# Seven products for tiles 2 and 3 as well, with prepared units kept in DRAM and retention beside the first two second layers

## The chip, the core and the metric

The kernel runs on one core of a Trainium2 chip. The metric is the device time of one execution in microseconds (us), median of the runs. TensorE (PE) multiplies, VectorE (DVE), ScalarE (ACT) and GpSimd (POOL) do the elementwise work, SyncE (SP) issues most transfers; POOL issues some too.

## The reference: what is computed

A retention layer over 4 batches, 8 heads, 768 tokens and head size 64 is followed by two feed-forward networks over the 3072 tokens:

```python
for t in range(S):                                   # retention, per head
    state = gamma * state + outer(k[t], v[t])
    y[t] = q[t] @ state / sqrt(D)
x = y as (3072, 512)
h = x @ w_in                                         # 512 -> 2048
g = where(h >= 1, h, where(h <= -1, 0, (h + 1)**2 / 4))
x = g @ w_out                                        # 2048 -> 512
out = ((x @ w1) * (x @ w2) @ w3) @ w_out2            # 512 -> 1024 -> 1024 -> 512
```

The weights arrive as 64-bit floats.

## The kernel before, in words

**Tiles.** The 3072 tokens are six tiles of 512 (a tile is one chunk of 128 tokens of each of the four batches). Retention of a chunk is one piece of scores on TensorE (`qk_ops`), a mask on VectorE, and one piece of values (`pv_ops`), which also brings the chunk's keys times values for the next state. Its result is the tile's x.

**Precision.** Every product of float32 values is made of three: each operand is split into a high and a low part (`plan_split`: a ScalarE copy gives the high part, a VectorE subtraction the low one), and `mm3` multiplies high by high, low by high and high by low. The 64-bit weights are converted on ScalarE and VectorE first (`convert`: a raw load, two ScalarE and four VectorE instructions).

**First layer, direct** (`plan_h`, tiles 0 to 3). For each of 16 blocks f of 128 hidden features, four blocks of x by `mm3`, that is twelve products of 128x512, then the gate: two ScalarE and one VectorE instruction on `r`. For tiles 0 to 3 (`LATE = 4`) the gated block is stored to DRAM (`g_d`, from POOL), loaded again (from SP) when its second layer comes, and split.

**First layer, seven products** (`plan_x_pair`, `plan_hu`, tiles 4 and 5). Two tiles and two blocks f form a 2x2 block product that is done with seven products of half the depth in place of eight (Strassen's scheme, in Winograd's form). The operands of x are sums and differences of the two tiles (`xops`, 14 buffers of the pool `w`); the operands of the weights are a *unit*, made from two blocks of w_in by sums on VectorE and splits (`plan_unit`, in the two buffers `xh` and `xl`). One unit n gives blocks 2n and 2n + 1 for both tiles. Tile 4's gate goes straight to its split; tile 5's blocks wait in `g_last`.

**Second layer** (`plan_y`). y of a tile sums over the 16 blocks f into four banks, twelve products a step. Tile 0 takes the converted w_out (`wo0`), which is also stored split (`wo_d`); later tiles load it back. Tiles 3 and 2 share one load a step. After step 15 the four banks are evacuated to DRAM (`plan_evac`).

**Second network.** w1, w2 and w3 are converted in the background and stored (`background`), w3 and w_out2 are multiplied into one matrix (`plan_w3o`, after tile 5's second layer), and the rest works by pairs of tiles (`plan_ab`, `plan_out`). The change does not touch that last part.

**Order.** The list `pe` gives TensorE's order by hand. A planner (`Plan`) lets each instruction of the other engines be issued in the order of its due time, taken back from the TensorE steps that need it, with the buffers of each pool counted; `bound` and `floor` move a due time. TensorE may take one of the next `AHEAD = 12` entries of its list if an earlier one is not ready. In time: retention of chunks 0 and 1 and h of tiles 0 and 1, with chunk 2 near the end; h of tile 2 alternating with y of tile 0; h of tile 3 alternating with y of tile 1, with chunks 3 to 5 between; y of tiles 3 and 2; the units of tiles 4 and 5 with y of tile 4 two steps behind; y of tile 5; w3 with w_out2; the pairs.

Of the kernel before, what the change touches and what calls it, by code (L numbers as in the profile page):

```python
# [15 lines left out]
P = 128  # L16
# [12 lines left out]
LATE = 4  # L29
PAIR = 4  # L30
KEEP = 260.0
DIRECT = 0
FEW = 4
# [17 lines left out]
class Op:  # L51
    def __init__(self, eng, cost, fn, size=0.0):
        self.eng, self.cost, self.fn, self.size = eng, cost, fn, size
        self.deps, self.after, self.vals = set(), [], []
        self.due = self.bound = float("inf")
        self.pos = self.end = None
        self.floor = -float("inf")
        self.store = False

    def lag(self):  # L60
        return self.size / 335.0 + 2.0 if self.size else 0.1


class Plan:
# [72 lines left out]
    def emit(self, begin):  # L137
# [18 lines left out]
        while done < len(self.ops):  # L156
# [71 lines left out]
def retention_then_two_ffns(  # L228
# [36 lines left out]
        (i, f): dram.tile([P, TT], F32, name=f"g_d{i}_{f}") for i in range(LATE) for f in range(NF1)  # L265
# [23 lines left out]
    def new_r(name):  # L289
# [10 lines left out]
    def convert(width, load, finish, after=(), bound=None, floor=-1e9, to=None):  # L300
# [22 lines left out]
        if to:  # L323
            words = lambda: to.ap.rearrange("p h w -> p (h w)").bitcast(U32)
        else:
            to, words = u, lambda: u.ap
        plan.op("DVE", 0.17 + 0.53 * s, lambda: nc.vector.scalar_tensor_tensor(
            out=words(), in0=odd(), scalar=0xC0000000, in1=u.ap,
            op0=ALU.bitwise_and, op1=ALU.bitwise_or), r=[raw, u], w=[to], bound=bound)
        finish(to)  # L330
# [77 lines left out]
    for f, n in [(0, 1), (1, 1)] + [(f, 2) for f in range(2, NF1, 2)]:  # L408
        convert(512 * n, load_rows(w_out[f // 2][:, f % 2 * 512:f % 2 * 512 + 512 * n]), finish_wo(f, n))
# [10 lines left out]
    background += [(load_rows(w3t[j]), [("w3", j), ("w3", NF2 + j)]) for j in range(DIRECT, NF2)]  # L420
# [20 lines left out]
    def new_ps(c):  # L441
        if c < 3:
            return Val("pe", lambda: psum["e"].tile([P, 2, 512], F32, tag="pa", name="pe"))
# [5 lines left out]
    def chunk(b, c):  # L449
# [10 lines left out]
        if c < 3:  # L460
# [3 lines left out]
        else:  # L464
            v_ = Val("v", lambda: att.tile([P, H, D], F32, tag="v", name="v"))
            k_ = Val("k", lambda: att.tile([P, H, D], F32, tag="k", name="k", bufs=1))
# [5 lines left out]
        ps = new_ps(c)  # L472

        def scores():
            q_t, k_t = q_at(), kT_at()
            for p in range(NP):
                for h in range(2):
                    r = slice(64 * h, 64 * h + 64)
                    nc.tensor.matmul(
                        out=ps.ap[:, h, p * C:(p + 1) * C], lhsT=k_t[r, p, :], rhs=q_t[r, p, :],  # L480
# [3 lines left out]
        qk = qk_ops[b, c] = plan.op("PE", 0.95, scores, w=[ps], use=[q_, kT_], after=[lq, lk])  # L484
# [6 lines left out]
        plan.op("DVE", 1.25, lambda: nc.vector.tensor_tensor(  # L491
            out=a_at().rearrange("p h a t -> p (h a) t"),
            in0=ps.ap.rearrange("p h (a t) -> p (h a) t", a=NP),
            in1=mask.rearrange("p h a t -> p (h a) t"), op=ALU.mult,
        ), r=[ps], w=[a])
# [49 lines left out]
        if c >= PAIR:  # L545
# [49 lines left out]
    hs, gs, h_ops, y_ops = {}, {}, {}, {}  # L595

    def plan_h(i, f):
# [13 lines left out]
        if i < 2:  # L611
# [8 lines left out]
        kept = r  # L620
        if i < LATE:
            d = Val(None, None)
            plan.op("POOL", 1.0, lambda: nc.gpsimd.dma_start(out=g_d[i, f], in_=r.ap), r=[r], w=[d], size=256)
            kept = Val("st", lambda: new_st("g"))
            plan.op("SP", 0.43, lambda: nc.sync.dma_start(out=kept.ap, in_=g_d[i, f]), r=[d], w=[kept], size=256)
# [12 lines left out]
    def keep_win(f, after, bound):  # L638
# [5 lines left out]
            r=[w], w=[t], after=after, bound=bound).floor = bound - 20.0  # L644
        plan.op("POOL", 0.6, lambda: nc.gpsimd.dma_start(
            out=win_d[f // 2][:, 512 * (f % 2):512 * (f % 2) + 512], in_=t.ap), r=[t], w=[d], size=256).floor = bound - 18.0

    def plan_unit(u, src, kept, after=()):
# [3 lines left out]
        plan.op("SP", 0.45, lambda: nc.sync.dma_start(out=u.ap, in_=src), r=kept, w=[u], size=512, after=after)  # L652
# [17 lines left out]
    def unit_tiles():  # L670
        return [xpool.tile([P, NK, TT], F32R, tag=t, name="unit") for t in ("xh", "xl")]
# [13 lines left out]
    def plan_x_pair():  # L685
        for kb in range(2):
            x4, x5 = xs[PAIR, kb], xs[PAIR + 1, kb]

            def operand(name, x, h):
                t = xops[kb, name] = Val("w", lambda: new_w("xop"))  # L690
# [23 lines left out]
    g_last = [Val("g5", lambda: late[0].tile([P, 2, 512], F32, tag="wc", name="g5", bufs=NF2)) for _ in range(NF1 // 2)]  # L714
    hu_ops = {}

    def plan_hu(n):
        uh, ul = plan_unit(
            Val("u", lambda: cpool.tile([P, 1024], F32, tag="u", name="u")),
            win_d[n], [win_kept[2 * n], win_kept[2 * n + 1]])  # L720
# [3 lines left out]
        ops = hu_ops[n] = []  # L724

        def product(name, where, first):
            def fn():
                w = views((uh.ap, ul.ap))[name]
                for kb in range(2):
                    x = xops[kb, name].ap  # L730
# [7 lines left out]
            ops.append(plan.op("PE", 1.362, fn, r=[uh, ul, xops[0, name], xops[1, name]],  # L738
# [8 lines left out]
        def gate(f, src, src_at, second):  # L747
# [4 lines left out]
            if second:  # L752
                g = g_last[f // 2]
# [7 lines left out]
            gs[PAIR, f] = g, plan_split(g, r, (slice(None),))  # L761
# [25 lines left out]
    def y_banks(i, beside):  # L787

        if not beside:
            vals = [Val("acc", lambda: psum["acc"].tile([P, TT], F32, tag="acc", name="y1acc")) for _ in range(NK)]  # L790
            return [(v, lambda v=v: v.ap) for v in vals]
        hs = [Val("h", lambda: ps_h.tile([P, TT], F32, tag="h", name="y1acc")) for _ in range(2)]
        pair = Val("pa", lambda: psum["a"].tile([P, 2, 512], F32, tag="pa", name="y1acc"))
        return [*((v, lambda v=v: v.ap) for v in hs), *((pair, lambda j=j: pair.ap[:, j]) for j in range(2))]

    def plan_y(tiles, f):

        if tiles[0] == 0:
            w = wo0[f]
        else:  # L800
            w = Val("wo", lambda: new_wo("wo"))
            plan.op("SP", 0.45, lambda: nc.sync.dma_start(out=w.ap.bitcast(F32), in_=wo_d[f]),
                    r=[wo_kept[f]], w=[w], size=512)
        for n, i in enumerate(tiles):
            if f == 0:
                banks[i] = y_banks(i, n < len(tiles) - 1)
            if i == PAIR + 1:
                g = Val("wo", lambda: new_wo("g"))
                plan_split(g, g_last[f // 2], (slice(None), f % 2))
            else:  # L810
                g, _ = gs.pop((i, f))

            def fn(i=i, g=g):
                for m, (_, at) in enumerate(banks[i]):
                    mm3(
                        at(), w.ap[:, 0, m * P:(m + 1) * P], w.ap[:, 1, m * P:(m + 1) * P],
                        g.ap[:, 0, :], g.ap[:, 1, :], f == 0, f == NF1 - 1,
                    )

            y_ops[i, f] = plan.op("PE", 2.724, fn, r=[g, w], w=list(dict.fromkeys(v for v, _ in banks[i])))  # L820
        if f == NF1 - 1:
            for i in tiles:
                for m, (v, at) in enumerate(banks[i]):
                    if 0 < i < PAIR:
                        if m % 2 == 0:
                            st = Val("w", lambda: wpool.tile([P, 2, 512], F32, tag="w", name="y1st"))
                        y1_stored[i, m] = plan_evac(y1_d[i][m], v, at, m, st, lambda st=st, m=m: st.ap[:, m % 2, :])
                    else:
                        st = Val("st", lambda: new_st("y1st"))
                        y1_stored[i, m] = plan_evac(y1_d[i][m], v, at, m, st, lambda st=st: st.ap)  # L830
# [7 lines left out]
    def plan_evac(dst, ps, at, m, st, st_at):  # L838
        done = Val(None, None)
        plan.op("ACT" if m % 2 else "DVE", 0.63, lambda: evacuate(st_at(), at(), m), r=[ps], part=[st, done])  # L840
# [19 lines left out]
    def plan_w3o(u):  # L860
        hf, j = divmod(u, NF2)
        if j == 0:
            banks["w3", hf] = y_banks(None, False)
# [5 lines left out]
        def fn():  # L869
            for m, (_, at) in enumerate(banks["w3", hf]):  # L870
                mm3(
                    at(), t.ap[:, 0, m * P:(m + 1) * P], t.ap[:, 1, m * P:(m + 1) * P],
                    t2.ap[:, 0, :], t2.ap[:, 1, :], j == 0, j == NF2 - 1,
                )

        w3_ops[u] = plan.op("PE", 2.724, fn, r=[t, t2], w=[v for v, _ in banks["w3", hf]])
        if j == NF2 - 1:
            for m, (v, _) in enumerate(banks["w3", hf]):
# [121 lines left out]
    with tc.manual_schedule():  # L1000
# [39 lines left out]
        for i in range(LATE):  # L1040
            for f in range(NF1):
                plan_h(i, f)
        for tiles in ((0,), (1,), (3, 2)):
            for f in range(NF1):
                plan_y(tiles, f)
        for f in range(2):
            keep_win(f, [y_ops[1, f]], KEEP + 9.0 * f)
        plan_x_pair()
        for n in range(NF1 // 2):
            plan_hu(n)  # L1050
        for i in (PAIR, PAIR + 1):
            for f in range(NF1):
                plan_y((i,), f)
# [24 lines left out]
        pieces = [x[b, 2] for b in range(B) for x in (qk_ops, pv_ops)]  # L1078
        lagging = 0
        for f in range(2, NF1):  # L1080
# [6 lines left out]
            if f >= NF1 - 3:  # L1087
                pe.append(pieces.pop(0))
        for f in range(lagging, NF1):
# [177 lines left out]
```

## Time and profile before

| | |
|---|---|
| median of 3 runs | 1025.09 us (1024.82 to 1025.96) |
| the profiled execution | 1026.57 us |
| its span | 1024.8 us |
| mean granted TensorE clock | 0.998 |

The span runs from the first to the last instruction in the profile; the profiled execution's time is 1.8 us longer. TensorE's products are pipelined: one shows as 0.39 us while the next starts 0.23 us after it. So the starts tell the cost, not the durations. An instruction's idle time before it stands in brackets with what ended it.

### The profile page before, as it was taken

What the parts mean: (1) busy time and instruction counts of PE and PEld (TensorE: products, weight loads), DVE (VectorE), ACT (ScalarE), POOL (GpSimd) and SP (SyncE); (2) the same over time, 40 slices, a digit from 0 to 9 for tenths busy, and PEclk for the clock granted to TensorE, in tenths of its full rate; (3) what the DMA queues carried; (4) which work ended last, traced back from release to release, by engine and by line L of the source; (5) the groups of instructions that cost most, each with busy time, mean ns of one, the idle gap of its engine ahead of it and who ended that gap; (6) DMA issues with size and microseconds to landing.
All of it is one profiled execution on the core that took longest, in us unless ns stands there. A gap on an engine that the chain in (4) does not pass through costs nothing.

```text
span 1024.8 us, 14489 instructions
## 1 busy us (share of the span) xinstructions
PE 1004.5 (98%) x5444; PEld 819.0 (80%) x5444; DVE 691.0 (67%) x1053; ACT 503.1 (49%) x845; POOL 96.0 (9%) x125
## 2 busy tenths in 40 slices
PE   6899999999999999999999999999999999999998
PEld 4777878878887788888888787888888888888886
DVE  6787569843656476687776867576884778747750
ACT  2467556632434454357766744444452445434430
POOL 2122332222323200000000000000000000000000
PEclk9999999999999999999999999999999999999999
DMA  9998959956998878864545784111321120311002
GB/s 269 261 272 252 330 177 365 365 194 207 374 343 304 313 265 294 318 213 163 185 185 211 254 300 159 44 39 42 113 89 66 42 103 32 134 41 42 21 4 79
DMA packets 71483, 191.23 MB, mean 187 GB/s; under 512 B 8946, under 2 KB 9330, under 8 KB 69492
## 3 DMA queue, kind: packets, MB, share of 16 engines
q1 hardware_dynamic: 63536, 164.39, 47.2%
q0 software_dynamic: 7584, 25.70, 6.5%
q8 instruction: 43, 0.70, 0.3%
q14 instruction: 28, 0.23, 0.1%
q10 hardware_dynamic: 292, 0.20, 0.1%
HBM read 139.93 MB, written 50.33 MB: 186 GB/s over the span
## 4 chain that ended last, share of the span: by engine, by line
PE 93%; DMA 3%; DVE 1%; ACT 1%; issue 1%; SPq 0%; ACTq 0%; DVEq 0%
PE bank_a L934 13%; PE y1acc L276 10%; PE y1acc L277 10%; PE y1acc L278 10%; PE bank_b L934 6%; PE hps L276 6%; PE hps L278 5%; PE hps L277 5%; PE oacc L982 4%; PE oacc L981 4%; PE oacc L983 4%; PE bank L733 4%; PE banks L733 3%; PE bank_c L934 3%; DMA raw<-in_w_in_dram 2%; PE pa L532 2%
## 5 line engine op out<-in xcount | busy, mean ns | idle before, releaser
L276 PE MATMUL y1acc<-g,wo 128*128 128x512 f32 x384 | 151.3, 394 | 1.1 <-ACT g L337 0.6
L278 PE MATMUL y1acc<-g,wo 128*128 128x512 f32 x384 | 149.7, 390 | 0.4 <-DVE g L339 0.4
L277 PE MATMUL y1acc<-g,wo 128*128 128x512 f32 x384 | 149.6, 390 | 0.0
L934 PE MATMUL bank_a<-yop,unit 128*128 128x512 f32 x576 | 145.7, 389 | 0.0
L934 PEld LDWEIGHTS bank_a<-yop,unit 128*128 128x128 f32 x576 | 108.1, 188 | 22.5
L276 PE MATMUL hps<-xh,win 128*128 128x512 f32 x256 | 102.8, 402 | 4.0 <-DVE r L618 2.1
L278 PE MATMUL hps<-xl,win 128*128 128x512 f32 x256 | 100.7, 393 | 0.0
L277 PE MATMUL hps<-xh,win 128*128 128x512 f32 x256 | 100.6, 393 | 0.0
L942 ACT COPY c<-bank_a 128x512 f32<-128x512 f32 x72 | 42.3, 587 | 98.0 <-PE bank_a L934 95.7
L615 ACT ACTIVATE r<-hps 128x512 f32<-128x512 f32 x64 | 38.2, 597 | 106.3 <-PE hps L278 104.9
L276 PEld LDWEIGHTS y1acc<-g,wo 128*128 128x128 f32 x384 | 72.1, 188 | 18.7 <-ACT g L337 1.1
L278 PEld LDWEIGHTS y1acc<-g,wo 128*128 128x128 f32 x384 | 72.1, 188 | 15.8 <-DVE g L339 0.8
L277 PEld LDWEIGHTS y1acc<-g,wo 128*128 128x128 f32 x384 | 72.1, 188 | 14.4
L337 ACT CAST g<-g 128x512 fp32r<-128x512 f32 x80 | 48.7, 620 | 65.8 <-PE y1acc L278 57.4
L618 DVE SCALAR_TENSOR_TENSOR r<-hps,r 128x512 f32<-128x512 f32 x64 | 43.9, 687 | 53.2 <-ACT r L617 52.4
L658 DVE TENSOR_TENSOR unit<-unit_w,unit 128x512 fp32r<-128x512 f32 x96 | 59.0, 622 | 28.3 <-ACT unit L656 27.9
L981 PE MATMUL oacc<-wc,p 128*128 128x512 f32 x192 | 74.7, 389 | 0.0
L982 PE MATMUL oacc<-wc,p 128*128 128x512 f32 x192 | 74.7, 389 | 0.0
L983 PE MATMUL oacc<-wc,p 128*128 128x512 f32 x192 | 74.7, 389 | 0.0
L934 PE MATMUL bank_b<-yop,unit 128*128 128x512 f32 x288 | 73.1, 389 | 0.0
L656 ACT CAST unit<-unit_w 128x512 fp32r<-128x512 f32 x96 | 53.6, 568 | 28.4 <-PE bank_b L934 14.6
L934 PEld LDWEIGHTS bank_b<-yop,unit 128*128 128x128 f32 x288 | 54.1, 188 | 11.2
(166 smaller groups left out, 1789.9 us busy)
## 6 DMA issues: line engine op xcount, KB each, us to landing
wo<-wo_d SPq DMA_DIRECT2D x64, 512.0 KB, 5.6
g_d<-r POOLq DMA_DIRECT2D x64, 256.0 KB, 4.8
g<-g_d SPq DMA_DIRECT2D x64, 256.0 KB, 5.3
unit_w<-sp_wab SPq DMA_DIRECT2D x24, 512.0 KB, 3.4
wo_d<-wo POOLq DMA_DIRECT2D x16, 512.0 KB, 7.3
raw<-in_w_dram SPq DMA_DIRECT2D x16, 512.0 KB, 6.4
raw<-in_w3t_dram SPq DMA_DIRECT2D x8, 1024.0 KB, 7.3
raw<-in_w_in_dram SPq DMA_DIRECT2D x28, 256.0 KB, 7.9
```

The costliest lines, as they stand in the source:

```text
L276: nc.tensor.matmul(out=ps, lhsT=lh, rhs=rh, start=first, stop=False)
L277: nc.tensor.matmul(out=ps, lhsT=ll, rhs=rh, start=False, stop=False)
L278: nc.tensor.matmul(out=ps, lhsT=lh, rhs=rl, start=False, stop=last)
L337: plan.op("ACT", 0.63, lambda: nc.scalar.copy(out=dst.ap[:, 0, :], in_=at()), r=r, w=[dst, hi], use=use, bound=bound)
L618: plan.op("DVE", 0.7, lambda: nc.vector.scalar_tensor_tensor(out=r.ap, in0=ps.ap, scalar=1.0, in1=r.ap, op0=ALU.max, op1=ALU.min), r=[ps], ...
L656: plan.op("ACT", 0.18 + 0.00088 * (b - a), lambda: nc.scalar.copy(out=hi(), in_=u.ap[:, a:b]), r=[u], part=[v, done])
L658: plan.op("DVE", 0.15 + 0.00106 * (b - a), lambda: nc.vector.tensor_tensor(out=lo(), in0=u.ap[:, a:b], in1=hi(), op=ALU.subtract), r=[u, d ...
L733: nc.tensor.matmul(out=at[where](), lhsT=l, rhs=r, start=first and kb + k == 0, stop=kb == 1 and k == 2, skip_group_check=True,)
L934: nc.tensor.matmul(out=vals[where].ap, lhsT=l, rhs=r, start=first and kb + k == 0, stop=kb == 1 and k == 2, skip_group_check=True,)
L981: nc.tensor.matmul(out=ps.ap, lhsT=lh, rhs=wh, start=(f == 0), stop=False)
L982: nc.tensor.matmul(out=ps.ap, lhsT=lh, rhs=wl, start=False, stop=False)
L983: nc.tensor.matmul(out=ps.ap, lhsT=ll, rhs=wh, start=False, stop=(f == NF2 - 1))
```

## The change

- `LATE` goes; the direct first layer is left for tiles 0 and 1. Tiles 2 and 3 take the seven products too: `plan_x_pair(i)` and `plan_hu(i, n)` run for i = 2 and i = 4.
- In the pass for tiles 2 and 3 a unit is prepared as before and both its buffers are stored to DRAM (`store_unit`, seven parts of 256 KB); in the pass for tiles 4 and 5 it is loaded ready made (`load_unit`).
- x of tiles 4 and 5 is stored to DRAM when it is complete and loaded again for its operands (`x_again`).
- Retention of tiles 2 and 3 stands between the steps of y of tile 0, of tiles 4 and 5 between the first 14 steps of y of tile 1. The scores of these chunks go to the two banks `h` in place of one double bank, and their mask is two instructions; `k` gets a second buffer.
- Order after that: units of tiles 2 and 3 with the last two steps of y of tile 1 and all of tile 2; eleven steps of tile 3; units of tiles 4 and 5 with the last five steps of tile 3 and tile 4; tile 5.
- y of tiles 2 and 3 no longer share their loads of w_out: each tile from 1 to 5 loads all 16.
- The first and last step of a sum over four banks is four entries, one for each bank (`by_bank`).
- `r` is taken from the pool of ten only for f < 8, from the pool of three otherwise.
- The conversions get other due times: w_out from 86 us on (`W_OUT`, `STEP`); w1, w2 and w3 as 4, 2 and 10 in the three stages from the first units on (`JOBS`). A unit's steps are `fixed`: TensorE does not reach past one to a later entry.

```diff
-LATE = 4
-KEEP = 260.0
-DIRECT = 0
-FEW = 4
+W_OUT = 86.0
+OWN_R = 8
+STEP = 4.5
+JOBS = (4, 2, 10)
+SLACK = 24.0
+LEAD = 6.0
+HEAD = 7.0
+HOLD = 5
+HOLD1 = 2
...
-                    cands = [o for o in pe[:AHEAD] if not left[o]]
+                    stop = next((k for k in range(1, min(AHEAD, len(pe))) if pe[k].fixed), AHEAD)
+                    cands = [o for o in pe[:stop] if not left[o]]
...
-        "k": 1, "a": 1, "sbd": 5, ...
+        "k": 2, "a": 1, "sbd": 5, ...
...
-        if i < 2:
+        if f < OWN_R:
             r = Val("wo", lambda: wpool.tile([P, TT], F32, tag="wo", name="r", bufs=10))
         else:
             r = Val("r", lambda: new_r("r"))
...
+    def store_unit(n, tiles):
+        kept = unit_kept[n] = []
+        for t, d, k in zip(tiles, unit_d[n], (4, 3)):
+            d_val = Val(None, None)
+            plan.op("SP", 0.45, lambda t=t, d=d, k=k: nc.sync.dma_start(out=d, in_=t.ap[:, 0:k, :].bitcast(F32)),
+                    r=[t], w=[d_val], size=256 * k).store = True
+            kept.append(d_val)
+
+    def load_unit(n):
+        tiles = []
+        for tag, d, k, kept in zip(("xh", "xl"), unit_d[n], (4, 3), unit_kept[n]):
+            t = Val(tag, lambda tag=tag: xpool.tile([P, NK, TT], F32R, tag=tag, name="unit"))
+            plan.op("SP", 0.45, lambda t=t, d=d, k=k: nc.sync.dma_start(out=t.ap[:, 0:k, :].bitcast(F32), in_=d),
+                    r=[kept], w=[t], size=256 * k).lead = LEAD
+            tiles.append(t)
+        return tiles
...
+    def x_again(c, kb):
+        d, t = Val(None, None), Val("w", lambda: wpool.tile([P, 2, 512], F32, tag="w", name="xs"))
+        first = xs[c, kb]
+        plan.op("SP", 0.45, lambda: nc.sync.dma_start(out=x_d[c, kb], in_=first.ap),
+                r=[first], w=[d], size=512).store = True
+        plan.op("SP", 0.45, lambda: nc.sync.dma_start(out=t.ap, in_=x_d[c, kb]), r=[d], w=[t], size=512).lead = LEAD
+        return t
...
-    def plan_hu(n):
-        uh, ul = plan_unit(
-            Val("u", lambda: cpool.tile([P, 1024], F32, tag="u", name="u")),
-            win_d[n], [win_kept[2 * n], win_kept[2 * n + 1]])
+    def plan_hu(i, n):
+        if i < PAIR:
+            uh, ul = plan_unit(
+                Val("u", lambda: cpool.tile([P, 1024], F32, tag="u", name="u")),
+                win_d[n], [win_kept[2 * n], win_kept[2 * n + 1]])
+            store_unit(n, (uh, ul))
+        else:
+            uh, ul = load_unit(n)
...
+    def by_bank(apart, sums, r, ps):
+        if apart:
+            return [plan.op("PE", 0.681, lambda m=m: sums(m), r=r, w=[ps[m]]) for m in range(NK)]
...
-        for f in range(NF1):
-            pe.append(h_ops[2, f])
-            if 8 < f < 15:
-                pe.append(pieces.pop(0))
-            pe.append(y_ops[0, f])
...
+        def beside(tiles, ys, every):
+            pieces = [x[b, c] for c in tiles for b in range(B) for x in (qk_ops, pv_ops)]
+            for n, y in enumerate(ys):
+                pe.extend(y)
+                k = int((n + 1) * every) - int(n * every)
+                pe.extend(pieces[:k])
+                del pieces[:k]
+        def units(i, ys):
+            for n in range(NF1 // 2):
+                for j, o in enumerate(hu_ops[i, n]):
+                    o.fixed = True
+                    pe.append(o)
+                    if j in (1, 3) and ys:
+                        pe.extend(ys.pop(0))
+            for y in ys:
+                pe.extend(y)
+        starts = [len(pe)]
+        y = lambda i, a=0, b=NF1: [y_ops[i, f] for f in range(a, b)]
+        beside((2, 3), y(0), 1.0)
+        beside((4, 5), y(1, 0, NF1 - HOLD1), 16 / (NF1 - HOLD1) + 0.01)
+        starts.append(len(pe))
+        units(2, y(1, NF1 - HOLD1) + y(2))
+        starts.append(len(pe))
+        for x in y(3, 0, NF1 - HOLD):
+            pe += x
+        starts.append(len(pe))
+        units(PAIR, y(3, NF1 - HOLD) + y(PAIR))
+        last_jobs = len(pe)
+        starts.append(last_jobs)
+        for x in y(PAIR + 1):
+            pe += x
```

## Rows read from the trace of the kernel before

**Rows 1.** The page: busy time by engine, and the span in 40 slices.

```profile
PE 1004.5 (98%) x5444; PEld 819.0 (80%) x5444; DVE 691.0 (67%) x1053; ACT 503.1 (49%) x845; POOL 96.0 (9%) x125
...
PE   6899999999999999999999999999999999999998
```

**Rows 2.** The page: the chain that ended last, shares by engine.

```profile
PE 93%; DMA 3%; DVE 1%; ACT 1%; issue 1%; SPq 0%; ACTq 0%; DVEq 0%
```

**Rows 3.** What TensorE waited for: us in total, times, longest.

```profile
PE rows_ps L1012 <- DMA rows<-in_c_decay_dram: 2.6, 1, 2.6
...
PE y1acc L276 <- ACT y1st L834: 1.7, 2, 1.2
...
PE y1acc L276 <- ACT g L337: 0.6, 1, 0.6
...
PE y1acc L278 <- DVE g L339: 0.4, 1, 0.4
```

**Rows 4.** Timeline of TensorE: an h step's first product, and the next step's.

```profile
170.31 0.39 PE L276 MATMUL hps<-xh,win 128*128 128x512 f32 x1
...
173.03 0.39 PE L276 MATMUL y1acc<-g,wo 128*128 128x512 f32 x1
```

**Rows 5.** The chain in order of time: start, us, one product of a unit.

```profile
450.21 1.36 PE banks L733 x6
```

**Rows 6.** Groups of TensorE instructions by line: count, busy, mean ns, idle before.

```profile
L276 PE MATMUL hps<-xh,win 128*128 128x512 f32 x256 | 102.8, 402 | 4.0 <-DVE r L618 2.1 <-ACT xh L575 1.8
L733 PE MATMUL bank<-xop,unit 128*128 128x512 f32 x192 | 47.6, 389 | 0.0
L733 PE MATMUL banks<-xop,unit 128*128 128x512 f32 x144 | 36.5, 389 | 0.0
```

**Rows 7.** Timeline of TensorE: first h step of tile 2, first sums of tile 5.

```profile
148.15 0.50 PE L276 MATMUL hps<-xh,win 128*128 128x512 f32 x1 [1.14 <-ACT xh L575]
...
573.30 0.47 PE L276 MATMUL y1acc<-g,wo 128*128 128x512 f32 x1 [0.50 <-ACT y1st L834]
```

**Rows 8.** Timeline of TensorE: one score piece and one value piece between products.

```profile
303.73 1.16 PE L479 MATMUL pa<-q,kT 64*128 64x128 f32 x16
...
310.17 0.39 PE L278 MATMUL hps<-xl,win 128*128 128x512 f32 x1
312.91 0.39 PE L277 MATMUL y1acc<-g,wo 128*128 128x512 f32 x1
```

**Rows 9.** Transfers by tensor: count, KB each, median us from issue to landing.

```profile
wo<-wo_d SPq DMA_DIRECT2D x64, 512.0 KB, 5.6
raw<-in_w_out_dram SPq DMA_DIRECT2D x7, 1024.0 KB, 7.7
```

**Rows 10.** Stretches: busy time of each engine, clock, transfer share, GB/s.

```profile
60.00:140.00 80.00, 79.25 (x509) 63.88 (x506) 55.88 (x81) 49.94 (x76) 22.93 (x32) 1.00 0.87 277
140.00:160.00 20.00, 18.86 (x131) 14.79 (x130) 15.78 (x24) 11.97 (x19) 6.14 (x9) 1.00 0.54 182
160.00:200.00 40.00, 40.00 (x178) 33.12 (x177) 34.86 (x46) 28.91 (x43) 10.68 (x18) 1.00 0.98 387
...
440.00:573.00 133.00, 131.82 (x580) 108.22 (x578) 100.50 (x161) 93.72 (x164) 0.00 (x0) 1.00 0.52 188
```

**Rows 11.** VectorE: the timeline's rows for each kind, and the operands' group.

```profile
149.94 0.69 DVE L315 TENSOR_SCALAR u<-u 128x1024 f32<-128x1024 f32 x1
...
151.39 1.23 DVE L321 CUSTOM_DVE_ANT_0 u<-raw,u 128x2048 uint16<-128x2048 uint16 x1
...
L694 DVE TENSOR_TENSOR xop<-xs,xop x14: 681/684/692, 371.3 to 446.2; 128x512 fp32r<-128x512 f32 x14
```

**Rows 12.** Life of a gate buffer: ScalarE, POOL; landings from 86 to 140 us.

```profile
107.06 0.60 ACT L615 ACTIVATE r<-hps 128x512 f32<-128x512 f32 x1 [1.46 <-DMA g_d<-r]
...
109.47 0.54 POOL L623 DMA_DIRECT2D g_d<-r  x1 [2.23 <-DVE r L618]
...
DMA to landing us min/median/max: 2.3/4.7/8.4
```

More of the change, by code (lines that the diff above doesn't have):

```diff
@@ L264, in retention_then_two_ffns @@
     g_d = {
-        (i, f): dram.tile([P, TT], F32, name=f"g_d{i}_{f}") for i in range(LATE) for f in range(NF1)
+        (i, f): dram.tile([P, TT], F32, name=f"g_d{i}_{f}") for i in range(2) for f in range(NF1)
     }
@@ L490, in chunk @@
             a_at = lambda: a.ap
[L491 to L495, printed above, removed]
+        if c < 2:
+            plan.op("DVE", 1.25, lambda: nc.vector.tensor_tensor(
+                out=a_at().rearrange("p h a t -> p (h a) t"),
+                in0=ps[0].ap.rearrange("p h (a t) -> p (h a) t", a=NP),
+                in1=mask.rearrange("p h a t -> p (h a) t"), op=ALU.mult,
+            ), r=ps, w=[a])
+        else:
+            for h in range(2):
+                plan.op("DVE", 0.7, lambda h=h: nc.vector.tensor_tensor(
+                    out=a_at()[:, h], in0=ps_at(h).rearrange("p (a t) -> p a t", a=NP),
+                    in1=mask[:, h], op=ALU.mult,
+                ), r=[ps[h]], part=[a])
         eng, many, ve = ("DVE", 0.7, nc.vector) if c < 2 else ("POOL", 1.3, nc.gpsimd)
@@ L785, in retention_then_two_ffns, with y_banks, fn, plan_y @@
     banks, y1_stored = {}, {}
[L787 to L798, printed above, removed]
+    def y_banks():
+        return [Val("acc", lambda: psum["acc"].tile([P, TT], F32, tag="acc", name="y1acc")) for _ in range(NK)]
+    def by_bank(apart, sums, r, ps):
+        if apart:
+            return [plan.op("PE", 0.681, lambda m=m: sums(m), r=r, w=[ps[m]]) for m in range(NK)]
+        def fn():
+            for m in range(NK):
+                sums(m)
+        return [plan.op("PE", 2.724, fn, r=r, w=ps)]
+    def plan_y(i, f):
+        if i == 0:
             w = wo0[f]
@@ L821, in plan_y @@
-        if f == NF1 - 1:
[L822 to L830, printed above, removed]
+                    r=[wo_kept[f]], w=[w], size=512).lead = LEAD
@@ new lines, in plan_y, with sums @@
+        if f == 0:
+            banks[i] = y_banks()
+        if (i, 0) in g_last:
+            g = Val("wo", lambda: new_wo("g"))
+            plan_split(g, g_last[i, f // 2], (slice(None), f % 2))
+        else:
+            g, _ = gs.pop((i, f))
+        def sums(m):
+            mm3(
+                banks[i][m].ap, w.ap[:, 0, m * P:(m + 1) * P], w.ap[:, 1, m * P:(m + 1) * P],
+                g.ap[:, 0, :], g.ap[:, 1, :], f == 0, f == NF1 - 1,
+            )
+        y_ops[i, f] = by_bank(f in (0, NF1 - 1), sums, [g, w], banks[i])
@@ L1128, in retention_then_two_ffns @@
-        end_jobs = len(pe)
-        pe += [y_ops[PAIR, NF1 - 2], y_ops[PAIR, NF1 - 1]]
+        pe += [h_ops[1, f] for f in range(lagging, NF1)]
+        pe.append(changed)
+        def beside(tiles, ys, every):
[5 more added lines that the diff above has]
+                del pieces[:k]
+            assert not pieces
@@ new lines, in units @@
+        def units(i, ys):
+            for n in range(NF1 // 2):
+                for j, o in enumerate(hu_ops[i, n]):
[9 more added lines that the diff above has]
+        beside((4, 5), y(1, 0, NF1 - HOLD1), 16 / (NF1 - HOLD1) + 0.01)
```

227 lines of the change are left out of this document (91 added, 136 removed), and 2 rows, old and new, of the table plan.

## The prediction

> **What bounds the kernel now.** I read the page's totals and its 40 slices first [rows 1]: TensorE is busy 98% of the span, and from the third slice on every slice but the last has it at nine tenths or more; the mean granted clock of 0.998 is the upper of its two levels, 2.4 GHz. VectorE (67%) and ScalarE (49%) are far behind. The chain of waits says the same: 93% of what ended last is TensorE work, 3% transfers, 1% VectorE [rows 2]. Next, the list of what TensorE waited for [rows 3]: eleven entries, of which the first and the last and those used below are shown, sum to 16.3 us, the largest before the first product. So there is little waiting to remove; the time changes through the number of products, and through new waits. The profiled execution took 1026.57 us, its span 1024.8, the median of the runs 1025.09; I sum differences against the profiled one and put them on the median, 1.5 us lower.
>
> **The change, part by part.**
>
> *Products.* One h step is twelve products; it starts at 170.31 and the next step at 173.03, 2.72 us, so 0.2267 us a product [rows 4]. A seven-product unit gives two h blocks for two tiles from 7 x 6 products, each six taking 1.36 us [rows 5], the same 0.2267 each. The direct h products of four tiles are 3 x 256 = 768 [rows 6], so tiles 2 and 3 have 384. The seven products of tiles 4 and 5 are 192 + 144 = 336 [rows 6], and the new pass over tiles 2 and 3 has as many. 48 products go: 48 x 0.2267 = **-10.9 us**, all on the engine that sets the end.
>
> *Waits that go.* The first h step of tile 2 waits 1.14 us for its x to be split after the last chunk [rows 7]; that step is gone, and x of tile 2 is wanted only by the units. Two sums wait for the evacuation of the banks before them, 1.7 us together [rows 3]: tile 5's 0.50 [rows 7], those with w3 1.2; with first and last steps split by bank, bank 0 is evacuated while banks 1 to 3 still run, three quarters of a 2.72 us step. **-2.8 us.** The tail after the last unit (0.6 + 0.4 us, until the last gate's two halves are there [rows 3]) moves to the tail after tile 2's sums, where again two steps are left over; behind the units of tiles 4 and 5 five steps are left, enough cover. Net 0.
>
> *Retention, moved.* Sixteen chunks of tiles 2 to 5 now stand between the sums of tiles 0 and 1. A score piece shows 1.16 us, 1.3 with the re-entry into wide products; a value piece takes from 310.40 (0.23 after the product before it) to 312.68 (0.23 before the second after it), 2.3 us [rows 8]. They already stand between wide products, so 0. The VectorE mask becomes two halves, each no wider than a split of 0.68 [rows 11], and hides behind a 2.72 us step as before.
>
> *The stage of tile 0's sums* gets denser: 16 x 2.72 + 8 x 3.6 = 72.4 us, where these sums now share some 98 us with h of tile 2 (32 steps, six pieces). It begins where h of tile 1 and the chunks beside it end, now 148.15 - 1.14 = 147.0 [rows 7], less four chunks: 132.6. In it must move, if five of sixteen w_out units stand ready (ten buffers, two a step): 5.5 raw loads of 1 MB, 12 stores of w_out of 512 KB, 15 g loads and 32 chunk loads of 256 KB, 3 w_out reads, 2 g stores (sizes after [rows 9]): 26.5 MB, 366 GB/s. Now the stretch with the same conversions ran at 387 GB/s over 40 us, and 60 to 140 us at 277 [rows 10]. At 387 it takes 68.5 us and hides; at 277 it takes 95.7, +23.3 us. I go by the first row, as the traffic is the same, but let 10 us start at the 182 GB/s of 140 to 160 [rows 10]: 2.05 MB short, 5.3 us to make up, 3.9 of it covered. **+1.5 us** (0 to 23; no gain, since TensorE's own work is the floor of the stage). VectorE stands close behind: a conversion is two instructions of 0.69 and two of 1.23 [rows 11], 3.84; with four splits of 0.684 and a chunk's four instructions, none longer than a split, that is 9.3 us at most for two steps that last 9.0; with five units ready it is 5.5 x 5.2 + 15 x 0.684 + 8 x 2.7 = 61 of the 72 us.
>
> *The end of h.* From h step 8 on, the gate value is in a pool of three buffers, not ten. Eleven such steps follow each other at 2.72 us, so a buffer must come round in 8.16 us. Life of one: ScalarE starts at 107.06, the POOL store is issued at 109.47 [rows 12], 2.4 us, and lands 4.7 us later in the median, 8.4 at most: 7.1 to 10.8 us. **+0.5 us** (0 to 11 x 2.6/3 = 9.7); I stay near the median.
>
> *Queues.* SP gains eight pairs of stores and eight of loads of prepared units (seven of 256 KB to a pair), 16 reads of w_out, four stores and four loads of x, and loses the 32 loads of g of tiles 2 and 3, as POOL loses their stores. In the units of tiles 2 and 3 move eight reads of w_in (4.2 MB), the unit stores (14.7), 18 reads of w_out (9.4), four conversions (1 MB in, 512 KB out: 6.3), x both ways (4.2), two g (0.5) (sizes after [rows 9]): 39.3 MB in 8 x 9.52 + 18 x 2.72 + 1 = 126 us, 312 GB/s; in those of tiles 4 and 5 the unit loads (14.7), 21 reads of w_out (11.0), ten conversions (15.7): 41.4 MB in 8 x 9.52 + 21 x 2.72 = 133 us, 311. The stretch now has 188 [rows 10], and 387 was held for 40 us. A load of a unit has the 15 us of the unit before it to land; 0 (to +10, below).
>
> *x of tiles 2 and 3* needs 14 of 16 buffers while x of tile 5 still holds two until stored; its last operands come when the fifth and seventh product want them, some 10 us into the units. +0.5 (0 to 8, the length of a unit's first half). *x of tiles 4 and 5* can be prepared only when the earlier operands come free, from the last unit on: its 15 us, two steps of tile 2 (5), eleven of tile 3 (30). VectorE then has 22 x 0.684 = 15 us for it [rows 11], 13 splits of 0.684, two conversions of 3.84 and the last unit's own 10.6 (100.5 us now in the eight [rows 10], less four conversions, by eight): 42 of 50 us. **+1.0** (0 if it starts with that unit, 6 if only after it, reload included). And these units need no preparing, which frees VectorE for ten conversions.
>
> **Sum:** -10.9 - 2.8 + 1.5 + 0.5 + 0.5 + 1.0 = -10.2; 1026.6 - 10.2 = 1016.4 for a profiled run, **1015 us** for the median.
>
> **The rivals.**
>
> *A. Starved sums (slower).* The one mechanism by which it loses: tile 0's sums go at the pace of conversions and chunk loads. For it: the transfer engines are 87% busy from 60 to 140 us, and 277 GB/s was all they gave [rows 10]. Against it: 387 with the same traffic, and w_out can be ready earlier: now all 32 gate values of tiles 0 and 1 pass through the ten buffers that w_out needs, then only half. At 277 GB/s: 1015 + 22 = 1037. It decides from 72.4 + 11.7 = 84 us on, so below 26.5/84 = 315 GB/s.
>
> *B. The three gate buffers.* For: the 8.4 us landing; ScalarE waited for such a store even with ten buffers, 1.46 us [rows 12]. Against: the median leaves 1 us. At the longest landing: 1015 + 9 = 1024. The Trainium skill has a way for it to happen: "SBUF — State Buffer", section "A bandwidth-pool intuition that's wrong (but worth ruling out)", says that a transfer issued by GpSimd waits for descriptors while VectorE holds the shared port, 620 ns growing to about 3100. By that page, an estimate, each landing would be 2.5 us longer, 11 x 0.48 = 5.3 us in all and the time 1020; the trace's landings of 2.3 to 8.4 us [rows 12] neither show nor exclude it.
>
> *C. Late second x.* VectorE behind at the second units, +6 instead of +1: 1020. For: 84% demand leaves VectorE 8 us, and it runs in order, so that an operand queued behind a conversion waits 3.84. Against: the due times let conversions slip, and only the first product's operands are urgent.
>
> *D. Prepared units come too late.* Then the saving of products is taken back by DRAM: 1.3 us a unit, eight units, is all of the 10.2: 1025. For: a unit passes through DRAM at 1.75 MB where now 0.5 MB was read. Against: 311 GB/s is well under 387, and two buffers give 15 us.
>
> **Chances.** Forecast (1011 to 1019) 0.60; A 0.13; B 0.08; C 0.10; D 0.09. Within 0.2% (2 us, about what a measurement can tell) are a third of B and most of D: 0.09. Slower: A and a little of D, 0.14. Faster: 0.77. The floor, with no new wait, is 1025.1 - 13.7 = 1011.4, less 1.4 for orders that fall out better: 1010. Up to 1026 leaves A out, some 0.14, and 0.04 below: the range is 1010 to 1026.
>
> **What would show it.** Right: 5396 TensorE products in place of 5444 [rows 1] (some records may lack); tile 0's sums from about 133 to 206.5, then 14 x 2.72 + 4 x 3.6 + 4 x 3.1 = 65 us of tile 1 and the units of tiles 2 and 3 from 272 to 398 with no gap over 1.5 us but their tail; after 11 x 2.72 + 1 us the second units from 429, tile 5's sums near 563 (now 573.3 [rows 7]), w3 sums following without a gap. The list of waits has w_out or g before tile 0's sums with under 3 us in total, ScalarE's wait for gate stores at the end of h under 1 us of TensorE idle. A shows as tile 0's sums lasting over 84 us, B as gaps before h steps between 100 and 133 us, C as waits for the second x near 425, D as a gap at each unit after 429. Wrong altogether if the products are fewer and the time is not: then one of these waits is over 8 us.

## The result, and the profile after

The changed kernel takes **1015.50 us** (median of 4 runs, 1014.85 to 1017.01), the kernel before, on the same chip, 1025.37 (1024.82 to 1025.96): ratio 0.9906, 95% interval 0.9889 to 0.9923. The forecast was 1015.0. The profiled execution took 1017.01 us with a span of 1015.2; the three others had spans of 1013.1 to 1014.0 at a granted clock of 0.997 to 1.0 (0.996 in the profiled one).

The page after: busy time by engine, two of its lines over the 40 slices, and the shares of the chain of waits (against [rows 1, 2]).

```profile
PE 994.9 (98%) x5396; PEld 811.8 (80%) x5396; DVE 716.5 (71%) x1107; ACT 527.9 (52%) x899; POOL 75.6 (7%) x93
...
PE   7899999989999999999999999999999999999998
...
PEclk8999999999999999999999999999999999999999
...
PE 90%; DMA 4%; DVE 2%; issue 2%; ACT 1%; SPq 0%; POOLq 0%; POOL 0%; DVEq 0%; ACTq 0%
```

The 48 products are gone, TensorE is busy 9.6 us less, and the span is 9.6 us shorter. So the idle time has not changed in total; what it consists of has. Before 60 us it is 12.1 us in the profile before and 9.9 in this one (10.4 to 11.7 in those of the experiments, so these two happen to be the extremes), from 60 to 280 us it rose from 1.9 to 6.8, and from 280 to 1010 us it fell from 2.7 to nothing. That the total is the same is thus in part chance. All that TensorE waited for (us in total, times, longest; against [rows 3]):

```profile
PE hps L283 <- DVE r L633: 4.3, 7, 1.6
PE pa L547 <- POOL q L516: 3.0, 2, 1.5
PE rows_ps L1066 <- DMA rows<-in_c_decay_dram: 2.6, 1, 2.6
PE pe L547 <- DVE a L500: 2.2, 2, 1.5
PE pe L547 <- DVE qk L516: 1.5, 2, 1.2
PE y1acc L285 <- DVE g L342: 1.0, 1, 1.0
PE hps L283 <- ACT xh L590: 0.7, 1, 0.7
PE pe L487 <- DMA qk<-in_kT_dram: 0.6, 1, 0.6
PE pe L487 <- DVE q L516: 0.4, 1, 0.4
PE y1acc L283 <- ACT g L340: 0.4, 1, 0.4
```

These sum to 16.7 us, before to 16.3. The waits for an evacuation are gone, and the longest for x with them. The wait for r, the gate value, has doubled, and the wait for a q that GpSimd scales is new. For r before:

```profile
PE hps L276 <- DVE r L618: 2.1, 3, 1.4
```

The stretches (columns: bounds, length, busy us and instructions of each engine, granted clock, transfer share, GB/s; against [rows 10]) show where:

```profile
60.00:150.00 90.00, 87.51 (x408) 70.36 (x405) 77.71 (x104) 67.94 (x103) 26.98 (x42) 1.00 0.96 327
150.00:280.00 130.00, 125.69 (x1265) 98.53 (x1264) 82.64 (x130) 41.98 (x88) 36.52 (x33) 1.00 0.89 310
280.00:430.00 150.00, 149.99 (x661) 123.56 (x660) 111.27 (x181) 101.67 (x175) 0.00 (x0) 1.00 0.84 318
430.00:570.00 140.00, 140.00 (x619) 115.95 (x618) 101.27 (x139) 98.94 (x154) 0.00 (x0) 1.00 0.83 307
```

From 280 us to the end of tile 5's sums at 608.8 TensorE never stops: the prepared units and both sets of x come in time, at 307 to 318 GB/s. New idle time stands only before 280 us. One place is where the kept copies of the first weights are made (keep_win, now at 83 us, before at 260 us). TensorE's rows, then VectorE's and GpSimd's around them:

```profile
87.32 0.50 PE L283 MATMUL hps<-xh,win 128*128 128x512 f32 x1 [1.33 <-DVE r L633]
90.62 0.50 PE L283 MATMUL hps<-xh,win 128*128 128x512 f32 x1 [0.28 <-DVE r L633]
```

```profile
82.62 4.05 DVE L342 TENSOR_TENSOR win<-u,win 128x512 fp32r<-128x512 f32 x2
86.59 0.68 DVE L633 SCALAR_TENSOR_TENSOR r<-hps,r 128x512 f32<-128x512 f32 x1
```

```profile
83.55 2.55 POOL L659 TENSOR_TENSOR win<-win 128x512 f32<-128x512 f32 x2
```

Two splits of a weight take 4.05 us on VectorE while GpSimd adds for 2.55; the gate value r stands in line behind them, and TensorE behind r. The other place is the stage of tile 1's sums, at its start (the g is that of the third step) and its end:

```profile
215.53 0.67 PE L547 MATMUL pa<-q,sbd 64*64 64x128 f32 x16 [1.49 <-POOL q L516]
...
219.14 0.50 PE L283 MATMUL y1acc<-g,wo 128*128 128x512 f32 x1 [0.36 <-ACT g L340]
...
220.84 0.50 PE L285 MATMUL y1acc<-g,wo 128*128 128x512 f32 x1 [0.97 <-DVE g L342]
...
274.58 0.67 PE L547 MATMUL pa<-q,sbd 64*64 64x128 f32 x16 [1.50 <-POOL q L516]
```

### The profile page after: what moved, and what is told of

Read it like the earlier page. It is cut to its first block, busy times and chain, and to the rows that moved or that the text cites. A ratio compares the mean times of both kernels' runs of the same rounds, so it can differ in the third digit from the quotient of the medians.

```text
span 1015.2 us, 14423 instructions
## 1 busy us (share of the span) xinstructions
PE 994.9 (98%) x5396; PEld 811.8 (80%) x5396; DVE 716.5 (71%) x1107; ACT 527.9 (52%) x899; POOL 75.6 (7%) x93
## 4 chain that ended last, share of the span: by engine, by line
PE 90%; DMA 4%; DVE 2%; issue 2%; ACT 1%; SPq 0%; POOLq 0%; POOL 0%; DVEq 0%; ACTq 0%
PE bank_a L988 13%; PE y1acc L283 10%; PE y1acc L285 10%; PE y1acc L284 10%; PE bank L786 9%; PE banks L786 6%; PE bank_b L988 6%; PE oacc L1037 4%; PE oacc L1036 4%; PE oacc L1035 4%; PE bank_c L988 3%; PE pa L547 2%; PE hps L283 2%; PE hps L285 2%; PE hps L284 2%
## 5 line engine op out<-in xcount | busy, mean ns | idle before, releaser
L786 PE MATMUL bank<-xop,unit 128*128 128x512 f32 x384 | 95.3, 389 | 0.0
L786 PEld LDWEIGHTS bank<-xop,unit 128*128 128x128 f32 x384 | 72.0, 188 | 15.1 <-issue 0.2
L786 PE MATMUL banks<-xop,unit 128*128 128x512 f32 x288 | 73.1, 389 | 0.0
L786 PEld LDWEIGHTS banks<-xop,unit 128*128 128x128 f32 x288 | 54.0, 188 | 11.3
L283 PE MATMUL hps<-xh,win 128*128 128x512 f32 x128 | 52.1, 407 | 5.0 <-DVE r L633 4.3
L564 ACT COPY xs<-pa 128x256 f32<-128x256 f32 x32 | 11.0, 375 | 82.8 <-DVE state L577 45.8
```

The lines of the kernel that those rows point to most:

```text
L283: nc.tensor.matmul(out=ps, lhsT=lh, rhs=rh, start=first, stop=False)
L786: nc.tensor.matmul(out=at[where](), lhsT=l, rhs=r, start=first and kb + k == 0, stop=kb == 1 and k == 2, skip_group_check=True,)
```

## The experiments

Each kernel was compared with the kernel before on its own chip (medians 1024.98 to 1025.21 us). Ratios carry a 95% interval, and the one to set them against is 0.9906.

**Only the products.** The kernel before, with three of four blocks of x in tile 3's h steps: 48 products less, nothing else of the change. It leaves a quarter of that sum out.

```
depth = NK - 1 if i == 3 else NK
for kk in range(depth):
```

> The kernel before with the direct first layer of tile 3 cut to three of its four blocks of x: 48 products of 128x512 are left out of the computation, nothing else. Theory (what TensorE no longer has to multiply is the whole of the gain, at 0.2267 us a product): 1025.4 - 10.9 = 1014.5 us, a ratio of 0.9894, and no wait grows by more than 0.5 us. The changed kernel stands at 0.9906, so the rest of the change would then be worth +1 us net. Rival (a third of the gain of the changed kernel comes from its order and its banks, because in the stage with tile 3 other engines and the transfers set the pace): 1018 us or more, with new waits before steps of tile 3.

1014.84 us, 0.9894 (0.988 to 0.9908): 10.3 us for the 48, by the medians on its chip. From 60 us on its waits are those of the kernel before, within 0.3 us each. The change took 9.9 us by the same measure, so its rest is worth about nothing in sum: a loss of 0.4 us by the medians, 1.2 by the ratios, and the intervals overlap.

**The prepared units.** All eight units of both pairs are prepared from the weights, nothing is stored (`if i < PAIR` becomes `if True`, `store_unit` goes).

> The changed kernel without the prepared units in DRAM: the units of tiles 4 and 5 are prepared again from w_in, none is stored. Theory (keeping them in DRAM saves VectorE and ScalarE, which do not set the end; TensorE is hidden behind neither): VectorE has some 4.2 us more for each of eight units, 34 us on top of some 95 in 130; it just fits, and the time stays within 2 us of the changed kernel, 1015 to 1018, with 25 MB fewer through DRAM. Rival (that part is needed: with ten conversions beside them VectorE is behind): waits of units for their weights or of the gates of over 8 us in all between 425 and 560 us, 1024 us or more.

1016.81 us, 0.991 (0.9891 to 0.993). From 280 us on:

```profile
280.00:430.00 150.00, 149.99 (x660) 123.56 (x660) 116.23 (x191) 105.62 (x183) 0.00 (x0) 1.00 0.57 215
430.00:570.00 140.00, 139.73 (x616) 115.40 (x616) 122.52 (x191) 108.08 (x177) 0.00 (x0) 1.00 0.66 242
```

VectorE works 744.0 us in place of 716.5, the transfers drop to 215 and 242 GB/s, and TensorE does not notice. Storing units is neither gain nor cost: it trades VectorE time for traffic, and neither of them bounds.

**The gate buffers** (`OWN_R = 16`: every gate value in the pool of ten).

> The changed kernel with every gate value of tiles 0 and 1 in the pool of ten buffers, none in the pool of three. Theory (three buffers come round in time, since the store lands 4.7 us after its issue in the median: rival B of the prediction did not happen): the waits of first-layer steps for the gate between 95 and 140 us, 0.5 us in all in the changed kernel, change by less than 0.5 us, and w_out, which shares the ten, comes later: 1015.5 to 1018. Rival (the three buffers do cost): 1 to 3 us less, 1013.

1018.60 us, 0.9934 (0.9915 to 0.9953). The wait for r is still 4.4 us in 6 times, so the three buffers were not its cause. The time is a little above the expected 1018. Tile 0's sums came later, the first at 134.8 us in place of 115.46, and among them stand new waits of 0.95 us for g and 1.31 us for a state.

**The start of the w_out conversions** (`W_OUT` from 86 to 106).

> The changed kernel with the conversions of w_out due 20 us later. Theory (tile 0's sums are within some per cent of what the transfers give, 358 and 324 GB/s over 140 to 180 us, so that a later start cannot be made up): gaps before sums of tile 0 of 5 to 15 us in all, 1020 to 1030 us. Rival (the transfers have room there): under 2 us, 1015 to 1017.5, and GB/s over 160 to 200 us rises above 380.

1015.18 us, 0.9899 (0.988 to 0.9918): no difference. The theory fell: TensorE has no gap from 120 to 200 us. The rival's time came, but not its sign: 306 GB/s over 160 to 200 us, not above 380.

**First and last steps by bank** (`if apart:` becomes `if False:`).

> The changed kernel with the first and last step of each sum as one entry for all four banks again. Theory (the split by bank is worth the two waits for an evacuation of before, 0.5 and 1.2 us, and as much at each other transition of tile to tile): five to seven transitions at 0.5 to 1.2 us, waits of sums for evacuations of 3 to 6 us in the list, 1019 us, ratio 0.994. Rival (the order hides the evacuations anyway, as most of them were hidden before): under 1 us, 1016.

1022.52 us, 0.9967 (0.9954 to 0.998): 0.6%, 6 to 7 us, more than either expectation. Two waits for an evacuation are in the list, 2.2 us together: 1.71 us before the sums with w3, which the prediction named, and 0.50 us before tile 3's sums.

```profile
PE y1acc L283 <- ACT y1st L889: 2.2, 2, 1.7
```

Most of the rest arose before them, at the end of tile 1's sums. A value piece waited longer for VectorE, and behind that the clock was granted below its upper level (0.56 and 0.58 of it from 274 to 278 and from 278 to 282 us):

```profile
275.78 2.15 PE L547 MATMUL pa<-a,v 128*64 128x128 f32 x16 [2.46 <-DVE a L507]
```

```profile
260.00:280.00 20.00, 16.05 (x157) 12.24 (x150) 14.68 (x23) 7.33 (x16) 2.57 (x2) 0.86 0.84 328
280.00:300.00 20.00, 20.00 (x86) 16.46 (x86) 9.78 (x15) 12.04 (x20) 0.00 (x0) 0.97 0.63 219
```

VectorE's rows there, and then the row of the same mask in the changed kernel:

```profile
268.37 4.78 DVE L740 TENSOR_TENSOR xop<-xs,xop 128x512 fp32r<-128x512 f32 x6 [0.80 <-ACT xop L739]
...
275.04 1.28 DVE L507 TENSOR_TENSOR a<-qk_ps,mask 128x512 f32<-128x512 f32 x2
```

```profile
273.12 1.29 DVE L507 TENSOR_TENSOR a<-qk_ps,mask 128x512 f32<-128x512 f32 x2 [1.61 <-PE qk_ps L487]
```

The piece's scores were done at 271.2 us, but six operands of x and three more instructions stood ahead of its mask on VectorE; in the changed kernel the mask follows its scores at once. So the edit also shifted VectorE's order, and that is not a price of the evacuations. The span of the profiled execution is 6.8 us longer than that of the changed kernel, 5.0 us of it idle and 1.8 us busy time of TensorE.

**keep_win later.** Its additions wait for the last h step of tile 1 (`[h_ops[0, 8]]` becomes `[h_ops[1, 15]]`).

> The changed kernel with the two GpSimd additions that restore the first blocks of w_in moved from behind tile 0's step 8 to behind tile 1's step 15. Theory (in the changed kernel a VectorE split at 83.2 us took 3.45 instead of 0.68 us because it and the GpSimd additions, 83.55 to 86.1 us, held each other off; TensorE then waited 1.33 + 0.28 us for the gate): that split takes 0.7 again, the two waits near 87 and 90 us go, 1.6 us less than the changed kernel: 1013.9, ratio 0.989. A VectorE instruction next to the additions at their new place is stretched in its turn. Rival (the long split waited for something of its own, its data or a buffer): some VectorE instruction near 83 us still lasts over 2 us, time unchanged, 1015.5.

1028.76 us, 1.0028 (1.0014 to 1.0041). The two splits take 1.28 us together, as the theory has it, and the waits near 87 us shrank to 0.3, but a larger stall came at the end of h, of which these are the longest waits:

```profile
111.92 0.50 PE L283 MATMUL hps<-xh,win 128*128 128x512 f32 x1 [1.76 <-DVE r L633]
...
121.38 0.50 PE L283 MATMUL hps<-xh,win 128*128 128x512 f32 x1 [3.21 <-DVE r L633]
```

I first took GpSimd's queue for the cause: a k scaling that waited for its load stood ahead of two stores of gate values.

```profile
113.77 1.63 POOL L519 TENSOR_TENSOR k<-k,small 128x512 f32<-128x512 f32 x1 [5.12 <-DMA k<-in_k_dram]
115.36 1.12 POOL L640 DMA_DIRECT2D g_d<-r  x2
```

**The loads of g issued earlier** (they get the lead that the weight loads have), meant for the 1.4 us of g at 219 us.

> The changed kernel with the due time of each load of g taken 4 us earlier (lead 6 in place of 2, as the loads of w_out have). Theory (at the start of tile 1's sums g comes late only because its loads stand behind chunk loads on SP that wait for their buffers; 1.5 us before a value piece and 1.4 before the sums): these waits between 210 and 222 us fall under 1 us, 2 to 3 us less than the changed kernel: 1013 us, ratio 0.988. Rival (the transfers are at their limit there, so that what is taken earlier makes something else late): 1015 to 1016.5, with as much waiting elsewhere between 130 and 280 us.

1019.51 us, 0.9939 (0.9924 to 0.9955): slower than the changed kernel. Here, too, a wait of 2.71 us for r came up, at 116.87, and the clock was 0.90 from 100 to 120 us; a wait of 1.4 us for g stayed.

**Both of these, and the pieces moved** (by the edit that stands under "The pieces" below).

> The changed kernel with three waits addressed: the GpSimd additions behind tile 1's step 15, the loads of g due 4 us earlier, and of the sixteen pieces beside tile 1's sums the two that double up placed at the start and the middle instead of the middle and the end (the last value piece waits 1.5 us for GpSimd directly behind its scores). Theory (the waits add up: 1.6 + 2 to 3 + 1.5): 1009.5 to 1011 us, ratio 0.985. Rival (transfers or VectorE give them back): 1013 or more.

1030.50 us, 1.0051 (1.0033 to 1.007): the stall of the later keep_win again.

**Is it GpSimd's queue?** keep_win late as above, and the k scalings of chunk 2 held back, so that none can stand ahead of a store.

```
held = []
...
got = chunk(b, c)
held += got[2] if c == 2 else []
...
for o in held:
    if h_ops[1, 14] not in o.deps:
        o.deps.add(h_ops[1, 14])
        h_ops[1, 14].after.append(o)
```

> Edit: as the kernel with keep_win after h step (1, 15), and the k scalings of chunk 2 on GpSimd also wait for h step (1, 14). Theory (that kernel lost 13 us because a k scaling that waited 5.12 us for its load stood ahead of the gate values' stores on GpSimd's queue): no wait of over 1 us for r between 105 and 150 us, granted clock over 0.97 there, 1014 to 1018 us, ratio 0.989 to 0.993. Rival (the loss is of crowded transfers or of VectorE's order at the end of h, not of GpSimd's queue): waits for r of 1.5 to 3 us between 110 and 150 us stay, 1025 to 1030 us, ratio 1.000 to 1.005. Third: the held scalings come too late for tile 2's value products: a new wait of 1 to 3 us at 150 to 160 us, 1017 to 1020 us.

1035.14 us, 1.0095 (1.0079 to 1.011). My theory fell: no k scaling stands in the way now, and the stall is as long. The time lies above all three ranges; behind the stall there are also waits of 2.05 us for a state at 170 us and 1.31 us for a k at 193 us. ScalarE's rows, of this kernel and then of the one with keep_win later alone:

```profile
116.93 1.12 ACT L317 ACTIVATE u<-raw 128x1024 f32<-128x1024 f32 x1 [4.24 <-DMA raw<-in_w_out_dram]
117.94 0.59 ACT L630 ACTIVATE r<-hps 128x512 f32<-128x512 f32 x1
```

```profile
118.15 1.12 ACT L317 ACTIVATE u<-raw 128x1024 f32<-128x1024 f32 x1 [3.91 <-DMA raw<-in_w_out_dram]
119.17 0.59 ACT L630 ACTIVATE r<-hps 128x512 f32<-128x512 f32 x1
```

ScalarE stands before the first step of a w_out conversion whose raw weights have not landed, and the gate's first instruction stands behind it. The third kernel with a late keep_win has the same row (3.86 us at 118.36); the changed kernel and the one with earlier loads of g have no wait of ScalarE for raw weights between 85 and 150 us. So in these three the gate is late behind a conversion in ScalarE's order. Whether the planner put that conversion too early or its raw weights were loaded too late, and what such a kernel would take with the conversion alone moved, was not tried.

A second thing differs in all four. In the changed kernel 36 products of tile 0's sums run before 140 us, between the last h steps, the first nine from 115.46 us. With a late keep_win none of these sums starts before 142 us, so h steps follow each other and TensorE meets each late gate at once. In the kernel with earlier loads of g the first three products come at 122.16 us, so at 116.87, where it waits its 2.71 us, nothing stands between two h steps. What a late gate costs with the sums in their old places was not tried either.

**The additions on VectorE.** keep_win stays where the change has it; VectorE adds in place of GpSimd.

```
-        plan.op("POOL", 1.36, lambda: nc.gpsimd.tensor_tensor(
+        plan.op("DVE", 0.7, lambda: nc.vector.tensor_tensor(
```

> Edit: the two additions of keep_win (hi plus lo of an input weight pair) go from GpSimd to VectorE, at the same place in the order; their stores stay on GpSimd's queue. Theory (the 2.55 us of GpSimd's two additions beside VectorE's split of 83.22 us stretch that split from 0.68 to 3.45 us, and TensorE's waits of 1.33 and 0.28 us for r follow from it): VectorE gets 2 x 0.7 us more, no split over 1 us near 83 us, those two waits gone or under 0.3 us together; 1013.9 us, ratio 0.989 (1013.2 to 1015.0). Rival (TensorE's waits for r there come from the gate buffers or the crowded order, whoever adds): the waits stay, 1015.5 us, ratio 0.9906, or 1017 if VectorE's extra 1.4 us make r later still.

1014.13 us, 0.9889 (0.9873 to 0.9905), where 1013.9 was expected. VectorE's rows at the same place:

```profile
80.17 1.28 DVE L342 TENSOR_TENSOR win<-u,win 128x512 fp32r<-128x512 f32 x2
...
81.37 0.69 DVE L659 TENSOR_TENSOR win<-win 128x512 f32<-128x512 f32 x1
...
82.76 0.68 DVE L659 TENSOR_TENSOR win<-win 128x512 f32<-128x512 f32 x1
```

The same two splits take 1.28 us instead of 4.05. VectorE does 1.4 us more work and loses 2.8 us less, and TensorE's waits there shrink from 1.61 to 0.52, not under the 0.3 that was expected. The variants of the changed kernel agree: the two splits take 4.04 to 4.06 us in the seven that add on GpSimd at this place, 1.28 us in the five that do not.

**The pieces.** Score and value pieces of tile 1's stage move by under one sum.

```
k = int((n + 1) * every + 0.8) - int(n * every + 0.8)
```

> Edit: only the places of the score and value pieces of chunks 4 and 5 among tile 1's sums move by under one sum (rounded from 0.8 and not from 0), so that no piece stands directly behind the one it needs at the last places. Theory: the waits of 1.5 us for q at 215.53 and 274.58 us shrink to under 0.5 us each, 1013 to 1015 us, ratio 0.988 to 0.990. Rival (the waits move to other pieces, since the planner takes what is ready): 1015 to 1017 us, ratio 0.990 to 0.992.

1015.92 us, 0.991 (0.9895 to 0.9924): the rival; both waits for q stay at 1.5 us, since the planner pulls the pieces together again.

**Both.**

> Edit: the additions of keep_win on VectorE and the moved pieces, together. If both theories hold: 1012 us, ratio 0.987 (1011 to 1014). If neither: 1015.5 us, ratio 0.9906. If only the additions matter: 1013.9 us. A time over 1018 us would mean that the planner's order changed elsewhere.

1014.40 us, 0.9892 (0.9876 to 0.9908): only the additions matter. On one chip, with the moved pieces in both, GpSimd's additions cost 1015.92 - 1014.40 = 1.5 us, and without the moved pieces the gap to the changed kernel's ratio is 0.0017, 1.7 us. The intervals overlap; what carries the reading is the rows, where 1.61 us of waits became 0.52 and 4.05 us of splits 1.28. The kernel with VectorE's additions has the lowest median of all.

## Why the prediction held, point by point

*Products (-10.9).* Right: 5396, and 10.3 us by the run that has them alone. The stages came near their places: the units of tiles 2 and 3 at 276.2 us (272 expected), tile 5's sums at 565 (563). Starting from the list of waits, and finding little in it, was what made the total come out.

*Waits that go (-2.8).* Right: no wait for an evacuation is left, tile 5's sums run into those with w3 at 608.80 without a gap, and the 1.14 us for x is gone. Without the split by bank such waits are 2.2 us, near the 1.7 us that I took for them. The run without it loses 6 to 7 us, but most of the rest arose at 275 us, from VectorE's order and a lower clock, and prices no evacuation.

*Tile 0's sums (+1.5, rival A at 1037).* Not there: the stage has no gap at all. The step that failed is that this stage begins where h of tile 1 ends: the planner took tile 0's first sums between the last h steps, from 115 us, so the traffic had longer, and no 182 GB/s start occurred. The stage's rows:

```profile
120.00:140.00 20.00, 19.68 (x87) 15.96 (x86) 16.80 (x23) 15.07 (x24) 5.03 (x10) 1.00 0.95 339
140.00:160.00 20.00, 20.00 (x187) 15.93 (x186) 16.75 (x25) 11.22 (x19) 7.12 (x10) 1.00 0.97 358
160.00:180.00 20.00, 20.00 (x197) 15.73 (x196) 18.46 (x25) 10.01 (x17) 8.30 (x8) 1.00 0.93 324
180.00:200.00 20.00, 20.00 (x210) 15.61 (x211) 10.57 (x18) 4.51 (x10) 7.29 (x8) 1.00 0.92 322
```

I had put the need at 315 GB/s at least, and 322 to 358 came. That is what the kernel asked for and no limit of the transfers: conversions 20 us later leave no gap either.

*Three gate buffers (+0.5, rival B).* Not there: with ten buffers the wait for r is the same. Landings of the gate stores from 86 to 140 us did get longer, as the rival needs:

```profile
DMA to landing us min/median/max: 3.9/6.4/8.9
```

The median was 4.7 us [rows 12]. With the 2.4 us ahead of it a buffer lives 8.8 us, over the 8.16 of three steps. But the steps did not follow each other without a break, since tile 0's sums stand among them. The Trainium skill's figure for a store held up by VectorE ("SBUF — State Buffer", section "A bandwidth-pool intuition that's wrong (but worth ruling out)"), by which I had 1020, made no difference to the time that these runs show: the median landing grew by 1.7 us, where by that estimate each was 2.5 us longer.

*x of both pairs (+0.5 and +1.0, rival C) and the prepared units (rival D).* Neither occurred: there is no wait over 0.3 us between 280 and 608 us, with units stored or prepared twice.

*What the sum missed.* The four costs, 3.5 us, did not come, and costs I had not named took their place: 1.6 us of r behind VectorE's stretched splits, two waits of 1.5 us for q, 1.3 us for the g of tile 1's third step, 5.9 us in all. Part of this is balanced by the 2.2 us less idle time before 60 us, which is luck. keep_win I had not priced at all: my part on queues counted the instructions of SP and the stores of GpSimd, but not the two additions that move from 260 us, where sums stand between the h steps, to 83 us, where h steps follow each other and each needs VectorE's gate of an earlier one. The pieces I costed at 0 on the evidence of one stage [rows 8]; that the scaling of q on GpSimd, 1.3 us, stands between two pieces when no sum is ready to go there was not looked at. So the total of 1015 is right by its largest term, and by small errors of both signs in the rest.

## What to carry to other kernels

When TensorE is busy 98% of the span, count its products first: 48 x 0.2267 us told the result within 1 us, and the run that removed nothing but products showed it. For a moved step look at what is critical where it arrives, on every engine it touches. After a change that is meant to remove a stall read all in-order queues again: two plausible edits here lost 4 and 13 us against the changed kernel, and in both the order of the steps had shifted, on TensorE too.

## What the runs showed of the hardware

An addition of two SBUF tiles on GpSimd stops VectorE's two-input instruction rather than slowing it in proportion: 4.05 us for two splits that take 1.28, the difference of 2.77 being about the 2.55 us of GpSimd's two additions, which themselves ran at full pace (1.29 us was the shorter of the two in the kernel before; the longer, 2.21 us, ran beside two instructions of VectorE). The Trainium skill says so ("SBUF — State Buffer", section "SBUF: two separate sides"): VectorE with two SBUF inputs and GpSimd share a port pair, one holds it for the whole instruction and the other is blocked. The trace agrees. Who gets the pair the profile does not settle: by its starts the long split began at 83.22 us, GpSimd's addition at 83.55, and VectorE was the one held up. GpSimd is thus no free place for small work while VectorE is a step away from the critical path.

A stall costs more than its length here. With keep_win later the clock was granted at 0.83 of its upper level, 2.4 GHz, from 120 to 150 us, which follows the waits of 1.8 and 3.2 us and holds two more of 1.7 and 1.5:

```profile
120.00:150.00 30.00, 25.48 (x101) 19.57 (x102) 15.01 (x20) 15.25 (x23) 10.16 (x15) 0.83 0.55 189
```
